# How the second batch's keys and queries are turned round: by TensorE, or as 32x32 blocks by VectorE

## The chip, the cores and the metric

The kernel runs on one core of one Trainium2 chip. The metric is the device time of one execution in microseconds (us); the figure used is the median over several runs. A profiled execution of the same kernel supplies the trace.

## The reference

For each of 8 batches and 8 heads, 32 pack vectors first attend to 576 keys, and then 576 queries attend to the 32 packed results. The heads' outputs form 4608 tokens of 512 features, and each token goes through a feed-forward layer whose nonlinearity is a quotient of polynomials.

```python
def sm_attn(qq, kk, vv):
    s = scale * np.matmul(qq, kk.transpose(0, 1, 3, 2))
    s = s - np.max(s, axis=-1, keepdims=True)
    a = np.exp(s)
    a = a / (np.sum(a, axis=-1, keepdims=True) + 1e-09)
    return np.matmul(a, vv)
p_packed = sm_attn(p, k, v)           # p: 8 x 8 x 32 x 64, k, v: 8 x 8 x 576 x 64
out = sm_attn(q, p_packed, p_packed)  # q: 8 x 8 x 576 x 64
x = out.transpose(0, 2, 1, 3).reshape(4608, 512)
h = x @ w_in                          # 512 x 2048
P = a[0] + a[1] * h + a[2] * h**2 + a[3] * h**3
Q = 1.0 + abs(b[0]) * abs(h) + abs(b[1]) * h**2
return (P / (Q + 1e-6)) @ w_out       # 2048 x 512
```

The weights of the feed-forward layer arrive as 64-bit floats and are brought to 32 bits on the chip.

## The kernel before, in words

**Tiling.** The feed-forward work is cut into 128 units: 8 batches, two halves of 288 tokens, and 8 chunks of 256 hidden features. A unit (`hidden`, L814) makes two tiles `h` on TensorE, evaluates the quotient on ScalarE, VectorE and GpSimd (tiles `Y`, `U`, `sq`, `V`), and leaves the result in `gh` and `gl`; three units later `acc_block` (L893) multiplies it with `w_out` into `acc`. In batch 0 the attention output `AH` is kept in plain 32 bits, and the first 12 units use plain 32-bit results too. From batch 1 on, operands are kept as two rounded parts and TensorE takes three products. While batch 0 is in work, the 64-bit weight words are still arriving and are converted (`convert`, L429, on ScalarE and VectorE).

**Attention.** `attention(bb)` (L548) is a generator of 16 steps. Batch 0 runs before the first unit. The steps of batch bb + 1 are handed out among the units of batch bb (L949 to L953), so batch 1's attention shares the engines with batch 0's units and with the weight conversion. Its steps: keys turned so that head features lie on the partitions (`transposed`, L569, called at L584), scores of the packs against the keys, softmax, the product with `v` (L683), the packed result transposed into `ppT` (L732, L733), queries turned (L736), scores of the queries against the packs, and the second softmax, whose result is `AH`.

**Two ways to load and turn keys and queries.** `rows4(bb)` (L464) chooses, and it is true for batches 0 and 1 in the kernel before.

- True: one DMA for each group of four heads brings 512 rows of a head as 128 partitions x 4 consecutive rows (L528); the last 64 rows of each head come apart, in tile `r` (L477, L490), which lives in a buffer of the ring `AH`. TensorE transposes 128x128 blocks into PSUM, and ScalarE copies them to `kx` (L574 to L581, L589 to L593, L738 to L744). The pack softmax is taken over two separate ranges of keys and joined afterwards with correction factors on VectorE and ScalarE (L647 to L657, L728 to L731).
- False: each group of four heads comes through four DMAs of 144 KB into 32 partitions each, made of single rows of 256 bytes (L513 to L518). VectorE transposes 32x32 blocks straight into `kx`, one instruction of 128x576 for two heads of a group (L570 to L573). All 576 rows come together, so tile `r` is not needed, and the two ranges share one maximum (L604 to L624), so the correction factors go.

`v` follows the row order: two DMAs of 256 KB instead of one of 512 KB a group (L509 to L511), four of 32 KB instead of two of 64 KB for its last rows (L499 to L501).

**What sets the order.** Nothing is issued as it stands in the source. `Planner` (L32) records all operations, gives each a cost (L40 to L48), simulates the engines in a list scheduler for four rounds, and issues the best order found. Every engine then works through its own queue strictly in that order. All DMAs are issued from SyncE (SP). The planner reckons a DMA at 600 ns of issue and with a rate by the length of the contiguous run: 190 bytes a nanosecond from 256 bytes on, and 370 from 1 KB on. In the first 150 us of the plan, TensorE's idle time is filled with small products of a zero tile (L992 to L1009), which add nothing.

The profile shows nearly all work under L226, the planner's issuing line, so groups are told apart by tile names.

Of the kernel before, what the change touches and what calls it, by code (L numbers as in the profile page):

```python
# [257 lines left out]
def attention_rational_ffn(  # L258
# [202 lines left out]


    NAT, AH, AL, PPT = {}, {}, {}, {}
    rows4 = lambda bb: bb < 2  # L464

    def load(bb, what):
        if bb >= B:
# [573 lines left out]
```

## Time and profile before

| | |
|---|---|
| median of 3 runs | 786.12 us (785.88 to 786.27) |
| profiled execution | 788.12 us |
| its span, from first to last instruction | 786.0 us |
| mean granted TensorE clock | 0.987 of full speed |
| TensorE / VectorE / ScalarE / GpSimd busy | 745.8 / 693.2 / 657.8 / 453.6 us |
| moved by DMA | 56.03 MB, mean 71 GB/s |

The busy shares are averages over stages that differ. The span has a start of some 50 us in which weights and the first batches arrive, then batch 0's units beside batch 1's attention up to about 150 us, then seven more batches of about 89 us each.

### The profile page before, as it was taken

The numbers are of one execution on the slowest core, as the hardware profiler recorded it, in microseconds if no ns is written. First come the engines' busy times: TensorE is split into PE (matmuls) and PEld (weight loads), VectorE is DVE, ScalarE is ACT, GpSimd is POOL, SyncE is SP. The second block draws the span as 40 slices with busy tenths as digits, with TensorE's granted clock in tenths as the row PEclk, the third lists the DMA queues.
The fourth block names the chain that finished last, engine by engine and source line by source line (L and its number), as shares of the span: only waits on it lengthen the run. The fifth ranks groups of instructions, "written<-read, shape, count | busy, mean of one in ns | idle before, by whom it ended". The sixth has DMA issues, their size and how long they took to land.

```text
span 786.0 us, 14945 instructions
## 1 busy us (share of the span) xinstructions
PE 745.8 (95%) x5336; PEld 567.5 (72%) x5336; DVE 693.2 (88%) x1295; ACT 657.8 (84%) x1464; POOL 453.6 (58%) x448
## 2 busy tenths in 40 slices
PE   2679999999999999999999999999999999999997
PEld 1345555588778887678778887678787887778886
DVE  4899999998999789998999789998999789988873
ACT  5869978988896998888897898889798788998872
POOL 0012448757585665756686555756587556766663
PEclk9959999999999999999999999999999999999999
DMA  9984353023601155023601136023701132000001
GB/s 297 332 296 143 108 100 49 1 85 46 110 1 55 45 66 90 1 85 46 95 17 55 44 52 104 1 58 62 94 28 54 41 45 46 1 22 7 27 1 41
DMA packets 152027, 56.03 MB, mean 71 GB/s; under 512 B 122256, under 2 KB 141200, under 8 KB 151952
## 3 DMA queue, kind: packets, MB, share of 16 engines
q1 hardware_dynamic: 151952, 55.07, 30.7%
q8 instruction: 42, 0.69, 0.4%
q14 instruction: 33, 0.27, 0.1%
HBM read 45.62 MB, written 9.44 MB: 70 GB/s over the span
## 4 chain that ended last, share of the span: by engine, by line
PE 76%; ACT 10%; DVE 8%; DMA 4%; issue 1%; POOL 0%; SPq 0%; DVEq 0%; ACTq 0%
PE acc L226 38%; PE h L226 24%; PE at L226 14%; DVE Y L226 4%; ACT Y L226 2%; DMA nat<-in_k_dram 2%; DVE w L226 2%; ACT V L226 1%; ACT U L226 1%; ACT sq L226 1%; ACT kx L226 1%; ACT w L226 1%; DMA m<-in_moe_w_in_dram 1%; ACT m L226 1%; DVE small L226 1%
## 5 line engine op out<-in xcount | busy, mean ns | idle before, releaser
L226 POOL TENSOR_TENSOR U<-U,sq 128x576 f32<-128x576 f32 x128 | 184.1, 1438 | 109.1 <-ACT U L226 55.8
L226 PE MATMUL acc<-w,gh 128*128 128x512 f32 x736 | 239.3, 408 | 1.6 <-ACT gh L226 1.4
L226 PE MATMUL h<-AH,m 128*128 128x288 f32 x1024 | 201.1, 320 | 7.9 <-DVE Y L226 5.6
L226 PEld LDWEIGHTS h<-AH,m 128*128 128x128 f32 x1024 | 163.0, 191 | 45.8 <-DVE Y L226 22.6
L226 POOL TENSOR_TENSOR gl<-Y,gh 128x512 fp32r<-128x512 f32 x116 | 150.2, 1295 | 39.0 <-issue 14.3
L226 PEld LDWEIGHTS acc<-w,gh 128*128 128x128 f32 x736 | 131.8, 188 | 45.5 <-issue 11.8
L226 PE MATMUL acc<-w,gl 128*128 128x512 f32 x384 | 147.9, 412 | 0.0
L226 ACT ACTIVATE Y<-h,abS 128x288 f32<-128x288 f32 x256 | 126.3, 511 | 23.2 <-PE h L226 19.7
L226 ACT ACTIVATE sq<-h 128x288 f32<-128x288 f32 x256 | 107.0, 419 | 39.2 <-PE h L226 31.0
L226 DVE TENSOR_TENSOR Y<-Y,h 128x288 f32<-128x288 f32 x256 | 109.1, 444 | 26.3 <-ACT Y L226 9.7
L226 DVE SCALAR_TENSOR_TENSOR Y<-Y,abS,h 128x288 f32<-128x288 f32 x256 | 124.5, 504 | 2.2
L226 DVE SCALAR_TENSOR_TENSOR Y<-Y,abS,V 128x576 f32<-128x576 f32 x128 | 102.8, 803 | 23.6 <-ACT V L226 23.0
L226 ACT ACTIVATE U<-h 128x288 f32<-128x288 f32 x256 | 98.6, 424 | 9.8 <-PE h L226 4.7
L226 ACT ACTIVATE V<-U,one 128x576 f32<-128x576 f32 x128 | 98.4, 769 | 5.6 <-DVE Y L226 3.8
L226 PE MATMUL h<-AL,m 128*128 128x288 f32 x448 | 96.1, 295 | 0.0
L226 DVE SCALAR_TENSOR_TENSOR V<-U,V 128x576 f32<-128x576 f32 x128 | 96.0, 750 | 0.0
L226 PEld LDWEIGHTS acc<-w,gl 128*128 128x128 f32 x384 | 71.9, 188 | 23.9 <-issue 9.6
L226 DVE SCALAR_TENSOR_TENSOR Y<-V,Y 128x576 f32<-128x576 f32 x116 | 86.7, 748 | 1.9
L226 POOL COPY G<-Y 128x64 f32<-128x64 f32 x116 | 27.5, 237 | 102.6 <-DVE Y L226 95.6
L226 ACT ACTIVATE V<-V 128x576 f32<-128x576 f32 x128 | 84.8, 663 | 0.7
L226 PE MATMUL acc<-half,gh 128*128 128x512 f32 x240 | 78.4, 413 | 1.3 <-ACT gh L226 0.9
L226 ACT CAST gh<-Y 128x512 fp32r<-128x512 f32 x116 | 73.4, 632 | 6.0 <-DVE Y L226 5.5
(135 smaller groups left out, 984.1 us busy)
## 6 DMA issues: line engine op xcount, KB each, us to landing
w<-in_moe_w_out_dram SPq DMA_DIRECT2D x16, 512.0 KB, 4.6
out_dram<-half SPq DMA_DIRECT2D x15, 512.0 KB, 3.1
nat<-in_k_dram SPq DMA_DIRECT2D x48, 144.0 KB, 3.9
nat<-in_q_dram SPq DMA_DIRECT2D x48, 144.0 KB, 4.3
nat<-in_v_dram SPq DMA_DIRECT2D x24, 256.0 KB, 3.7
m<-in_moe_w_in_dram SPq DMA_DIRECT2D x8, 512.0 KB, 6.2
w<-in_moe_w_in_dram SPq DMA_DIRECT2D x8, 512.0 KB, 8.2
nat<-in_k_dram SPq DMA_DIRECT2D x4, 512.0 KB, 7.7
```

What stands on the lines that cost most here:

```text
L226: getattr(getattr(self.nc, engine), name)(*args, **kwargs)
```

## The change

One number changes. Batch 1 takes the second way of loading and turning keys and queries, which batches 2 to 7 already take; only batch 0 keeps the first.

```diff
-    rows4 = lambda bb: bb < 2
+    rows4 = lambda bb: bb < 1
```

`rows4` is asked in `load`, `transposed`, `attention` and in the order of the output rows (L912), so all of what is described under "False" above now holds for batch 1. The planner then makes a new order for the whole kernel.

## Rows read from the trace of the kernel before

**Rows 1.** Page, part 4: the chain that ended last, by engine
```profile
PE 76%; ACT 10%; DVE 8%; DMA 4%; issue 1%; POOL 0%; SPq 0%; DVEq 0%; ACTq 0%
```
**Rows 2.** Windows by stage: busy us (and count) by engine, clock, DMA share, GB/s
```profile
core 0: us, PE busy (x) PEld busy (x) DVE busy (x) ACT busy (x) POOL busy (x), PEclk, DMA share, GB/s
48.00:88.00 40.00, 35.68 (x225) 18.48 (x225) 38.14 (x61) 37.89 (x80) 13.33 (x9) 0.86 0.54 185
88.00:110.00 22.00, 20.70 (x152) 12.07 (x151) 21.95 (x42) 17.43 (x37) 8.51 (x7) 1.00 0.31 99
110.00:153.00 43.00, 43.00 (x210) 23.08 (x210) 40.19 (x82) 38.62 (x84) 31.70 (x27) 1.00 0.28 41
153.00:190.00 37.00, 37.00 (x343) 30.00 (x342) 32.77 (x65) 34.12 (x82) 22.31 (x24) 1.00 0.15 46
```
**Rows 3.** Chain in order of time, start: start us, us, what
```profile
29.66 9.84 DMA nat<-in_k_dram
40.00 5.30 DMA w<-in_moe_w_in_dram
47.62 2.96 DVE w L226 x3
53.79 4.22 PE h L226 x8
```
**Rows 4.** Chain in order of time, batch 1's attention
```profile
59.14 0.48 ACT kx L226
65.63 0.30 ACT kx L226
96.75 0.07 DVE small L226
109.50 0.27 DVE small L226
109.81 0.66 PE at L226 x4
111.53 0.44 PE at L226 x4
112.83 0.44 PE at L226 x4
114.24 0.87 PE at L226 x8
```
**Rows 5.** Timeline of SP: start us, us, issue, count
```profile
28.16 2.00 SPq L226 DMA_DIRECT2D nat<-in_k_dram  x2
30.21 2.08 SPq L226 DMA_DIRECT2D AH<-in_k_dram  x1
32.40 2.13 SPq L226 DMA_DIRECT2D pn<-in_p_dram  x3
34.57 0.42 SPq L226 DMA_DIRECT2D AH<-in_q_dram  x1
35.51 0.31 SPq L226 DMA_DIRECT2D pn<-in_p_dram  x1
37.10 0.31 SPq L226 DMA_DIRECT2D AH<-in_q_dram  x1
39.57 0.90 SPq L226 DMA_DIRECT2D w<-in_moe_w_in_dram  x2
...
101.33 1.22 SPq L226 DMA_DIRECT2D nat<-in_q_dram  x2
...
112.00 6.76 SPq L226 DMA_DIRECT2D nat<-in_k_dram  x8
```
**Rows 6.** DMA of 101 to 108 us, queue: packets, MB, share of 16 engines
```profile
q1 hardware_dynamic: 1632, 1.18, 47.3%
```
**Rows 7.** DMA of 112 to 122 us, the same line
```profile
q1 hardware_dynamic: 9344, 1.18, 106.2%
```
**Rows 8.** Tile nat on VectorE: ns min/median/max, first and last start
```profile
L226 DVE STREAM_TRANSPOSE kx<-nat x48: 732/767/773, 150.7 to 657.9; 128x576 f32<-128x576 f32 x48
```
**Rows 9.** Timeline of ScalarE: start us, us, operation, idle before and releaser
```profile
45.39 1.19 ACT L226 ACTIVATE w<-w 128x1024 f32<-128x1024 f32 x1 [4.87 <-DMA w<-in_moe_w_in_dram]
```
**Rows 10.** Timeline of VectorE, the same columns
```profile
44.91 0.77 DVE L226 STREAM_TRANSPOSE AH<-kx 128x576 f32<-128x576 f32 x1
47.62 0.69 DVE L226 TENSOR_SCALAR w<-w 128x1024 int32<-128x1024 int32 x1 [1.36 <-ACT win L226]
```

**Rows 11.** Timeline of TensorE: start us, us, operation, count
```profile
63.77 0.60 PE L226 MATMUL at<-ident,AH 128*128 128x128 f32 x4
...
72.60 0.67 PE L226 MATMUL at<-kx,small 64*32 64x256 f32 x16
...
108.93 0.27 PE L226 MATMUL at<-ident,nat 128*128 128x128 f32 x1
...
121.42 0.72 PE L226 MATMUL at<-kx,ppT 64*32 64x288 f32 x16
```

## The prediction

> **What bounds the kernel now.** I first read the chain of waits by engine [rows 1]: TensorE holds 76% of it, so over the whole span the kernel is a TensorE kernel. But the change touches batch 1's attention alone, which lies in the first 150 us, so I next read the busy time by stage [rows 2]. From 48 to 88 us ScalarE (37.89 of 40) and VectorE (38.14) are both nearly full; from 88 to 110 VectorE is busy 21.95 of 22 us; from 110 on TensorE is busy without a gap, 43.00 of 43 and 37.00 of 37, while VectorE still has 40.19 of 43 and only after 153 some air (32.77 of 37). Thus the stage into which VectorE work is to be put is the one stage where VectorE has no room. Third comes the chain in order of time. At the start it runs through a DMA: batch 1's keys take 9.84 us from issue to landing, the next weight words only then start, and take 5.30 us more [rows 3]; ScalarE idles 4.87 us for those words [rows 9]. In the middle it passes through a few pieces of batch 1's attention on ScalarE and VectorE, and from 109.81 us on it is TensorE [rows 4].
>
> **The change part by part.**
>
> *TensorE.* 40 transposes of 128x128 go: 16 for keys, 4 for the keys' last rows, and the same again for queries. Eight of them take 0.87 us on the chain [rows 4], 0.109 us each. The 20 for keys are over at 64 us [rows 11], where TensorE was not the limit: worth nothing. Those for queries start at 108.93 us, and from 109.81 on TensorE is the limit: 20 x 0.109 = 2.2 us off the chain, if VectorE keeps up. The score products change by slivers (64 columns become 32), which I cost at nothing.
>
> *ScalarE.* 11 copies from PSUM go. Only two of those for keys stand on the chain, 0.48 and 0.30 us [rows 4], 0.78 together. VectorE is as full as ScalarE there, so I count half, 0.4.
>
> *VectorE.* Eight block transposes come, at 0.767 us [rows 8]: 4 for keys, 3.07 us, and 4 for queries, 3.07 us. Off go four tiny operations of the joined softmax, each about 0.08 us of chain (a neighbour shows 0.07), and two scalings of 0.27 us [rows 4]: 4 x 0.08 + 2 x 0.27 = 0.86 us, all in the stretch where VectorE is the limit. Net +5.3 us of VectorE work between 45 and about 120 us.
>
> The keys' transposes have one gap to hide in, the 1.36 us before 47.62 us [rows 10], if the keys have landed. Bounds: 0 to +3.07; I take 3.07 - 1.36 = +1.7, because that gap is the only one near their landing.
>
> The queries' transposes fall at about 110 us. If VectorE gets behind there, +3.07; if it fits them into the 2.8 us left of 43 [rows 2] and TensorE stays the limit, -2.2. I take the middle, +0.45: both engines are over 93% busy, so neither row is nearer.
>
> *The DMAs.* Batch 1's issues on SP grow from 15 to 28: keys 2 to 8, queries 2 to 8, `v` 2 to 4 and its last rows 2 to 4, while the three of tile `r` go and the four of `p` stay. Eight key issues of this form take 6.76 us of SP's time; the present two with the one of `r` behind them take 4.08 [rows 5]. The transfer matters more. 1.18 MB in the present form (queries of batch 1 and four small pieces of `v`) held the 16 engines for 0.473 x 7 = 3.3 us [rows 6]; the same 1.18 MB in 256-byte rows (keys of batch 2) held them for 1.062 x 10 = 10.6 us [rows 7]. Batch 1's keys take 3.3 us for the bulk plus about 1.2 us for the 0.13 MB of `r` (10.6 / 9), 4.5 us in all; they will take 10.6, or 6.1 us more, at a time when weight words queue behind them.
>
> How much of it is felt? The weight words issued at 39.57 us stand eight issues behind the second key DMA (issued at 29.66), which landed just before, at 39.50 [rows 3, 5]: SP seems to wait for the landing of the DMA eight places ahead. With eight key DMAs and four of `p` in front, the words would wait for the fifth key DMA. If key transfers begin at 39.5 - 4.5 = 35 us, it lands at 35 + 5/8 x 10.6 = 41.6, 2.1 us later. Bounds: 0 if the planner puts the words first, +6.1 if they wait for all of it. I take +2.0. Everything behind it waits: ScalarE's idle time [rows 9], the conversion on VectorE, the first chunks' products.
>
> Queries are issued at 101.33 us [rows 5] and will land some 7 us later than now (10.6 - 3.3), at about 113; the first products with them run at 121.42 [rows 11], so I cost that at nothing; without that cover, the queries' transposes would hold up VectorE's queue (conversions and unit work behind them), up to 7 us. The next batch's keys come correspondingly later, with over 25 us to spare (their first transposes are at 150.7 [rows 8]).
>
> The Trainium skill, "DMA: Bandwidth & Descriptors", section "Why small descriptors are slow (HBM only)", puts the loss of 256-byte pieces at a fixed 3 cycles on 8, or 27%. That does not agree with the 3.3 and 10.6 us above, a factor of 3.2. By its figure, an estimate, the keys would cost about 3.3 x 1.27 = 4.2 us, no more than now, and the start term would be 0.
>
> *The sum.* Start +2.0, keys on VectorE +1.7, ScalarE's copies -0.4, small operations -0.86, queries +0.45: +2.9 us. On the profiled execution, 788.12 + 2.9 = 791.0 us. That execution is 2.0 us above the median of the runs, so the median should be 786.12 + 2.9 = 789.0.
>
> **The rivals.**
>
> *Faster: TensorE and ScalarE shed work and VectorE hides its own.* The planner puts the weight words ahead of the keys and finds room for the transposes. For it: the chain from 109.81 us on is all TensorE, and there is slack before keys are used (the scores come at 72.60 us [rows 11]). Against it: VectorE's 21.95 of 22 us [rows 2]. -2.2 - 0.78 - 0.86 = -3.8, so 782.3 us. The Trainium skill, "VectorE: DVE Perf Modes", section "Rules for kernel authors", says as much: for 32x32 blocks the VectorE transpose is the fastest. The trace has 0.767 us for 576 columns, 0.17 for each 128, against 0.109 on TensorE, so per column it is not faster here; what speaks for it is the copy that ScalarE saves.
>
> *Nothing seen: the costs cancel.* Start and keys are hidden, and VectorE's delay at 110 us eats TensorE's 2.2: 786 us, within 1 us.
>
> *Much slower: VectorE's queue is blocked by a DMA.* Place: the keys' transposes, ordered before batch 0's last softmax operations and the conversion (VectorE's transposes into `AH` at 44.91 us, `w` at 47.62 [rows 10]). The planner reckons 256-byte rows at 190 bytes a nanosecond, 6.2 us for 1.18 MB, where [rows 7] shows 10.6. VectorE then stands at its queue's head for up to 4.4 us, and `AH`, the conversions and all products of `h` behind it wait. It decides as soon as the second group's transposes are ordered before about 46 us (35 + 10.6). Price: the full start term 6.1 and the whole VectorE addition 5.3: +11, 797 us. Against it: in later batches no VectorE transpose of `nat` shows a wait for its DMA.
>
> That the change does not act as described I rule out: batches 2 to 7 show this form in the trace [rows 8]. The new order of the whole plan can move the rest by a microsecond; TensorE is saturated after 150 us, which leaves little to move.
>
> **How the numbers follow.** Forecast 789.0: chance 0.40 (0.32 of it slower by over 0.2%, 0.08 within). Faster rival 0.25 (0.23 and 0.02). Nothing seen 0.20 (0.14 within, 0.03 on either side). Much slower 0.15. A measurement of this kernel tells about 0.2%, 1.6 us, from no change. Hence faster 0.26, same 0.24, slower 0.50. The range goes from 782.0, just below the faster rival, to 796.0, just short of the worst sum; the forecast's own is 786 to 793 (each of its two positive terms at zero, or the start at 6.1).
>
> **What would show it.** In the profile after: SP issues eight key DMAs near 28 us and the words of 39.57 us come 2 us later, ScalarE's idle time for them grows from 4.87 to about 7 us. VectorE busy rises by 5 us, 4.4 us less of TensorE's transposes and some 4 us less of ScalarE's copies (8 of 0.48 and 0.30). The chain between 60 and 110 us turns from ScalarE to VectorE. TensorE's unbroken stretch starts later than 109.8 us. The forecast is wrong if the words go ahead of the keys, if VectorE's addition sits in gaps that the present order doesn't show, or if a wait for `nat` stands ahead of VectorE's work.

## The result, and the profile after

The changed kernel takes 790.84 us (median of 5 runs, 789.34 to 791.28) against 786.12 us before. The ratio is 1.0049, with a 95% interval of 1.0036 to 1.0061: slower by half a per cent, 4.7 us. The forecast was 789.0. The two profiled executions are 791.01 and 788.12 us, 2.9 us apart: the one before lay 2.0 us above the median of its runs, the one after 0.2. A few executions below (839 to 2526 us) ran in a slower state of the chip; they count in the medians given, not in the ratios, and the traced one of "keys only" is among them, so that kernel has no row in the table of units.

The page of the changed kernel, part 1 (busy us, share of the span, instructions) and part 4 (the chain by engine):

```profile
PE 742.0 (94%) x5308; PEld 563.3 (71%) x5308; DVE 701.0 (89%) x1297; ACT 653.8 (83%) x1452; POOL 453.8 (57%) x448
...
PE 74%; DVE 12%; ACT 8%; DMA 2%; issue 2%; SPq 1%; POOL 0%; ACTq 0%; DVEq 0%
```

VectorE rose by 7.8 us and ScalarE fell by 4.0, TensorE by 3.8; the chain moved the same way, VectorE from 8% [rows 1] to 12%. The same stages as in [rows 2], now after the change:

```profile
48.00:88.00 40.00, 30.00 (x178) 15.45 (x177) 38.80 (x62) 36.95 (x71) 13.34 (x9) 0.81 0.63 212
88.00:110.00 22.00, 20.70 (x149) 11.61 (x147) 21.17 (x31) 15.16 (x30) 6.26 (x4) 1.00 0.40 87
110.00:153.00 43.00, 41.33 (x195) 20.63 (x196) 42.74 (x85) 36.65 (x77) 30.59 (x25) 1.00 0.40 51
153.00:190.00 37.00, 36.80 (x267) 29.74 (x266) 34.01 (x66) 33.18 (x81) 23.93 (x25) 1.00 0.15 46
```

VectorE (third engine column) is busy 42.74 of 43 us between 110 and 153, where it had 40.19, and TensorE (first) is no longer without gaps there. TensorE's granted clock in the stage from 48 to 88 us fell from 0.86 to 0.81; two experiments below that lose 4.0 and 7.5 us had 0.89 in that stage, so their loss is not the clock's. The chain of the changed kernel in order of time (start us, us, what) shows the turn: TensorE's unbroken stretch, which began at 109.81 [rows 4], is now reached at 119.54, is lost again to VectorE at 130.53, and holds from 145.70 on. VectorE holds the chain from 92.17 us:

```profile
92.17 0.46 DVE Y L226
...
111.25 1.32 DVE w L226
...
119.54 2.81 PE acc L226 x6
...
130.53 0.46 DVE kx L226
...
144.50 1.16 DVE Y L226 x3
145.70 2.21 PE h L226 x8
```

The start, SP's timeline as in [rows 5], and the rows of ScalarE and VectorE that answer to [rows 9, 10] (start us, us, operation, count, idle before):

```profile
24.84 12.86 SPq L226 DMA_DIRECT2D nat<-in_k_dram  x7
37.74 1.32 SPq L226 DMA_DIRECT2D w<-in_moe_w_out_dram  x2
39.11 0.43 SPq L226 DMA_DIRECT2D nat<-in_k_dram  x1
39.65 2.57 SPq L226 DMA_DIRECT2D pn<-in_p_dram  x4
42.31 0.90 SPq L226 DMA_DIRECT2D w<-in_moe_w_in_dram  x2
```
```profile
44.39 1.15 ACT L226 ACTIVATE w<-w 128x1024 f32<-128x1024 f32 x1 [1.17 <-DMA w<-in_moe_w_out_dram]
```
```profile
45.62 2.10 DVE L226 STREAM_TRANSPOSE kx<-nat 128x576 f32<-128x576 f32 x3
48.13 0.46 DVE L226 TENSOR_TENSOR Y<-Y,h 128x288 f32<-128x288 f32 x1 [0.42 <-ACT sq L226]
48.51 0.77 DVE L226 STREAM_TRANSPOSE kx<-nat 128x576 f32<-128x576 f32 x1
```

The words issued at 39.57 us before come 2.74 us later. The first words of `w_out` moved much further: the planner has put seven of the key loads ahead of them, and they are issued at 37.74 us, where the kernel before has them ahead of its keys:

```profile
25.23 1.70 SPq L226 DMA_DIRECT2D w<-in_moe_w_out_dram  x2
```

VectorE's hole of 1.36 us [rows 10] is gone: key transposes stand in it.

Where the time was lost is best read unit by unit. Every unit has one first activation of `V` on ScalarE; the table gives how much later its start is than in the kernel before (us, from the timelines of ScalarE, one execution each; the last column is the last unit). The runs of the kernel before alone spread from 785.2 to 789.9 us on one chip, so a difference of one or two us between two rows can't be read.

```
unit               0     2     4     6     8    10    13    15    18    24   127
after            1.1  -1.6  -0.1   1.5   1.6   3.8   5.9   5.6   3.3   2.9   3.4
queries only     2.0   0.6   1.5   0.1   0.6   1.9   2.3   3.0   0.1   0.8   0.8
row loads       -1.0  -0.9   3.8   1.9   2.5   2.4   3.2   3.7   2.8   2.7   2.9
vector work     -0.9  -1.1   4.4   2.5   3.5   6.2   5.6   6.3   4.5   5.7   5.6
long key loads   2.3   1.7   5.1   1.6   1.8   4.0   3.6   3.3   2.1   2.7   2.4
after, words 1st 2.9   2.4   4.6   5.0   2.9   4.4   4.8   5.3   3.3   4.0   4.1
same order long  2.5   0.6   2.1   3.7   3.8   6.0   8.1   7.8   5.5   5.1   5.5
before, 2nd plan 0.2  -2.1  -2.2  -1.8  -3.0  -1.6  -0.7  -0.9  -4.0  -3.5  -3.1
```

In the changed kernel units 1 to 4 are not late. The delay builds up between units 4 and 13 (86 to 151 us), reaches 5.9 us, falls to 2.9 by unit 24, and stays near that. Every row of the table gains between units 15 and 18 (0.9 to 3.1 us), whatever its change: part of that fall belongs to the kernel before, or to its one traced execution.

How full VectorE is until unit 15 is told by one window per kernel, from 34 us to the start of that unit's activation. First the kernel before:

```profile
34.00:156.31 122.31, 112.37 (x678) 61.22 (x677) 116.24 (x213) 106.35 (x221) 54.55 (x43) 0.92 0.43 122
```
And after:
```profile
34.00:161.88 127.88, 111.33 (x665) 58.60 (x662) 125.27 (x219) 104.78 (x212) 54.56 (x43) 0.91 0.52 126
```

Before, VectorE was idle for 122.31 - 116.24 = 6.1 us of this stretch, after for 2.6. It is busy 9.0 us longer by then: 3.5 us of that went into idle time, 5.6 became delay. What it does more can be told by form (operation, count, busy us, mean ns). The groups of transposes and of one step of the weight conversion, first before, then after:

```profile
L226 DVE STREAM_TRANSPOSE kx<-nat 128x576 f32<-128x576 f32 x2 | 1.5, 767 | 0.0
L226 DVE SCALAR_TENSOR_TENSOR w<-w 128x1024 int32<-128x1024 int32 x11 | 13.8, 1264 | 0.0
```
```profile
L226 DVE STREAM_TRANSPOSE kx<-nat 128x576 f32<-128x576 f32 x11 | 8.2, 760 | 0.0
L226 DVE SCALAR_TENSOR_TENSOR w<-w 128x1024 int32<-128x1024 int32 x11 | 15.5, 1409 | 0.0
```

Nine more transposes (eight of batch 1, one of batch 2 that now comes before unit 15) are 6.7 us. The same eleven conversion steps took 1.7 us longer, which the forecast did not have; why they did is not shown.

### The profile page after: what moved, and what is told of

The parts are those of the page before. It is cut to its first block, busy times and chain, and to the rows that moved or that the text cites. A ratio compares the mean times of both kernels' runs of the same rounds, so it can differ in the third digit from the quotient of the medians.

```text
span 789.3 us, 14893 instructions
## 1 busy us (share of the span) xinstructions
PE 742.0 (94%) x5308; PEld 563.3 (71%) x5308; DVE 701.0 (89%) x1297; ACT 653.8 (83%) x1452; POOL 453.8 (57%) x448
## 4 chain that ended last, share of the span: by engine, by line
PE 74%; DVE 12%; ACT 8%; DMA 2%; issue 2%; SPq 1%; POOL 0%; ACTq 0%; DVEq 0%
PE acc L226 37%; PE h L226 24%; PE at L226 13%; DVE Y L226 5%; DVE w L226 3%; ACT Y L226 2%; DMA nat<-in_k_dram 2%; DVE small L226 1%; ACT U L226 1%; ACT sq L226 1%; DMA AH<-in_k_dram 1%; ACT kx L226 1%; DVE V L226 1%; SPq L226 1%; ACT V L226 1%
## 5 line engine op out<-in xcount | busy, mean ns | idle before, releaser
L226 PEld LDWEIGHTS acc<-w,gl 128*128 128x128 f32 x384 | 71.7, 188 | 26.0 <-issue 11.8
```

Source lines behind the costliest of these rows:

```text
L226: getattr(getattr(self.nc, engine), name)(*args, **kwargs)
```

## The experiments

Theory 1: VectorE's added work is the loss, because VectorE has no room in batch 0's stage. Theory 2: the loads in small pieces hold up the weight words. Theory 3: any new plan moves the time by as much. All ratios are against runs of the kernel before on the same chip. Except under "The same order", each kernel below also has a new order from the planner, so what it shows of a cost includes that of its order.

**Keys only.** A second switch for the queries, so that batch 1's keys alone take the new way.

```diff
-    rows4 = lambda bb: bb < 2
+    rows4 = lambda bb: bb < 1      # keys, v, pack softmax
+    rows4q = lambda bb: bb < 2     # queries, order of the output rows
```

> Only batch 1's keys (with v and the pack softmax) take the new way; its queries stay with TensorE. Theory 1 (VectorE has no room in batch 0's stage): +3.07 us of key transposes, less the 1.36 us gap before 47.6 us, less 0.86 us of small operations: +0.9, so 786 to 788 us. Theory 2 (the loads in small pieces): the keys are the ones that queue ahead of weight words, so most of the loss is here, 788 to 791. Theory 3 (the loss is only what any new plan gives): no number, as likely below as above 786.

Measured: 792.54 us, ratio 1.0063 (1.0048 to 1.0079). The whole loss is seen with the keys (and `v` and the pack softmax, which change with them). Theory 1's number (at most 788) is missed by over 4 us; theory 2's (up to 791) is just passed.

**Queries only.** The two bounds exchanged.

> Only batch 1's queries take the new way. Theory 1: 3.07 us more on VectorE at about 110 us, where it is full, and 2.2 us less on TensorE that cannot be used while VectorE is behind: 788 to 790 us. Theory 2: at 100 to 115 us the DMA engines are mostly free, so the loads cost nothing and TensorE's 2.2 us are gained: 784 to 786.

Measured: 787.67 us, ratio 1.0004 (0.9994 to 1.0014). The queries' part costs nothing that can be measured, between the two expectations. Units 13 to 15 are 2.3 to 3.0 us late, as theory 1 has it, and 0.8 is left by unit 24.

**Row loads, TensorE transposes.**

```diff
+        if bb == 1 and x != "v":
+            t = nat_ring.next()
...          # the four DMAs of the new way into t
+            NAT[bb, what] = t[:, 0 : 4 * NS * D].rearrange("p (h s d) -> p h s d", h=4, s=NS)
+            return
```

> The kernel before, but batch 1's keys and queries are loaded in the small pieces of the new way (8 DMAs of 144 KB each) while TensorE still transposes and ScalarE copies; what it then computes for batch 1 is in the wrong order. Theory 1: the loads are covered, 786 us within 1. Theory 2: the whole loss, 789 to 792.

Measured: 791.09 us, ratio 1.0050 (1.0037 to 1.0063): the loads, with no VectorE work added, cost nearly as much as the change (4.0 of 4.7 us). Theory 2's number. The loads of tile `r` (256 KB) stay in this kernel, which the change takes out. Its `w_out` words are late as in the changed kernel (issued from 37.71 us on). Until its unit 15, 3.7 us late, VectorE is idle for 125.96 - 117.82 = 8.1 us, 2.1 more than before, in waits for units that come late; the other 1.6 us are operations that took longer or were put earlier:

```profile
34.00:159.96 125.96, 111.53 (x681) 60.74 (x674) 117.82 (x216) 106.53 (x222) 54.80 (x43) 0.95 0.51 128
```
```profile
48.43 0.46 DVE L226 TENSOR_TENSOR Y<-Y,h 128x288 f32<-128x288 f32 x1 [2.55 <-ACT sq L226]
52.73 0.46 DVE L226 TENSOR_TENSOR Y<-Y,h 128x288 f32<-128x288 f32 x1 [2.29 <-ACT sq L226]
```

**VectorE work alone.** Each copy of batch 1's keys and queries into `kx` is preceded by a VectorE transpose into the same place.

```diff
+                if bb == 1:
+                    flat_n = NAT[bb, f"{x}{g}"].rearrange("p h s d -> p (h s d)")
+                    n = flat_n[:, 512 * r : 512 * r + 512].rearrange("p (j c) -> p j c", j=2)
+                    nc.vector.transpose(to[:, r, 2 * g : 2 * g + 2, :], n)
```

> The kernel before, with 8 VectorE block transposes of 128x512 added in batch 1's attention, 4 from the keys' tiles and 4 from the queries' (some 5.5 us of VectorE), whose results are overwritten; loads, TensorE and ScalarE as before. Theory 1: the whole loss or more, 790 to 792 us, because TensorE keeps its transposes. Theory 2: 786 within 1.

Measured: 794.63 us, ratio 1.0098 (1.0083 to 1.0112), 7.5 us: more than theory 1 asked. VectorE is full in the stages that follow:

```profile
48.00:88.00 40.00, 31.87 (x219) 16.61 (x218) 38.48 (x59) 36.64 (x76) 13.32 (x8) 0.89 0.54 180
88.00:110.00 22.00, 21.75 (x165) 12.45 (x158) 22.00 (x43) 16.84 (x35) 7.69 (x5) 1.00 0.33 105
110.00:153.00 43.00, 40.48 (x186) 20.95 (x185) 42.70 (x82) 35.99 (x76) 30.23 (x25) 1.00 0.25 40
```

So the loads alone lose 4.0 us and VectorE work alone 7.5, and the change, which has both, 4.7: they do not add. The comparison is not clean: the added transposes also delay ScalarE's copies behind them, which the changed kernel doesn't have, and TensorE keeps its transposes.

**Long key loads.** The changed kernel with batch 1's keys loaded per group in one DMA of 512 KB and two of 32 KB.

> The kernel after, but batch 1's keys are loaded in long pieces (per group one DMA of 512 KB and two of 32 KB); VectorE still does the block transposes, so what is computed for batch 1 is wrong. Theory 1 (VectorE's added work is the loss): no change against the kernel after, about 1.005 of before. Theory 2 (the key loads hold up the weight words): the loss goes, 0.998 to 1.001 of before. Both, as two ways to use up the same VectorE time: a part stays, 1.002 to 1.004.

Measured: 789.01 us, ratio 1.0017 (1.0004 to 1.0031): some two thirds of the loss go when the planner may reckon with cheap key loads. Its order is then another one: `w_out`'s first words stand ahead of the keys again.

```profile
25.41 1.71 SPq L226 DMA_DIRECT2D w<-in_moe_w_out_dram  x2
28.34 6.50 SPq L226 DMA_DIRECT2D nat<-in_k_dram  x6
```

So it is not shown whether the gain is the transfer's or the order's.

**Words first.** An edge for the planner: key loads of batch 1 wait for the issue of two sets of words. First on the kernel after, then on the one before.

```diff
+            if "in_k" in x.tensor.name and x.offset // (8 * 576 * 64) == 1:
+                edges[i].update(words)   # DMAs of w_out chunk 0 and w_in chunk 6
```

> The kernel after, with one edge added for the planner: batch 1's key loads are not issued before the weight words of the first w_out chunk and the seventh w_in chunk. The same work and the same bytes in another order on SP. Theory 1: as the kernel after, 1.005 of before. Theory 2: the words come in time, 0.998 to 1.001. Both: 1.002 to 1.004.

> The kernel before with the same added edge. Theory 1: no change, 1.000. Theory 2: its key loads hold up the words too (ScalarE idles 4.87 us for them), so 0.995 to 0.999. If another order of SP alone moves the time by half a per cent either way, theory 3 (any new plan) gains.

Measured: 793.04 us, ratio 1.0074 (1.0049 to 1.0100), and 789.90 us, ratio 1.0038 (1.0025 to 1.0050). Theory 2 in its simple form falls: with the words in front the time does not get better. The kernel before gets worse; the kernel after can't be told from 1.0049, as the intervals overlap. The second result speaks for theory 3 by its own expectation: an edge that adds no work, only another order, costs 0.38% (0.25 to 0.50), nearly as much as the change. In the first kernel, SP issues the keys from 41.46 us on, and VectorE takes their transposes at 56 to 63 us, in the full stage instead of the hole:

```profile
41.46 10.93 SPq L232 DMA_DIRECT2D nat<-in_k_dram  x8
```
```profile
56.42 1.43 DVE L232 STREAM_TRANSPOSE kx<-nat 128x576 f32<-128x576 f32 x2
...
61.94 1.42 DVE L232 STREAM_TRANSPOSE kx<-nat 128x576 f32<-128x576 f32 x2
```

**The same order, one cost removed.** These three keep the changed kernel's order instruction for instruction on every engine and exchange calls only when they are issued. The first reads one contiguous stretch per partition for each of the eight key DMAs; the second makes plain copies of the eight transposes; the third does both.

```diff
+            name, args = swap(engine, name, args)
             getattr(getattr(self.nc, engine), name)(*args, **kwargs)
```

> The kernel after with its order kept instruction for instruction; only the eight key loads of batch 1 read one contiguous stretch per partition instead of 36 pieces of 128 bytes (same 144 KB each, same target, wrong data). It takes the loads' form alone out, with no new plan. Theory 2: the loss goes, 1.000 of before or less. Theory 1: unchanged, 1.005. Both: in between, 1.002 to 1.004.

> The kernel after with its order kept instruction for instruction; only the eight block transposes of batch 1 become plain copies of the same 128x576 on VectorE, which I expect to take about half the time (some 3 us less VectorE work in all; the data are then not transposed). Theory 1: the time falls by nearly as much, to 1.001 to 1.002 of before. Theory 2: unchanged, 1.005.

> Both of the last two at once, the order kept. If the two costs add up: below before, 0.997 to 0.999. If they stand in for one another (a late load leaves VectorE a hole that the transposes fill), less than the sum of the two, 0.999 to 1.001.

Measured: 792.84 us, ratio 1.0070 (1.0058 to 1.0083); 792.20, ratio 1.0062 (1.0050 to 1.0074); 792.67, ratio 1.0067 (1.0054 to 1.0080). Not one of them gains, and the expectation for the third (at most 1.001) is missed whichever way the two costs combine. For the loads the answer is plain: with this order the form of the key loads is not what costs. The key issues go faster (seven in 8.52 us instead of 12.86), but words of `w_in` issued just ahead of them take 12.23 us to land, SP waits for them, and `w_out`'s are issued at 36.38, hardly earlier than 37.74 (first a line of the chain, then SP's timeline):

```profile
24.13 12.23 DMA w<-in_moe_w_in_dram
```
```profile
25.29 8.52 SPq L241 DMA_DIRECT2D nat<-in_k_dram  x7
36.38 1.63 SPq L241 DMA_DIRECT2D w<-in_moe_w_out_dram  x2
```

From unit 2 on this kernel's units are the changed kernel's shifted by 2.2 us, and its VectorE is as full, which fits a pace set by the order of VectorE's queue. The shift is not the loads': the kernel with copies, whose loads are the changed kernel's, lies 1.8 us behind it from unit 10 on. The changed kernel itself was not run beside these three. The second experiment failed to remove its cost. The copies came out nearly as long as the transposes (ns min/median/max), so it says nothing against theory 1:

```profile
L238 DVE COPY kx<-nat x8: 452/630/1181, 46.9 to 126.1; 128x576 f32<-128x576 f32 x8
```

**Other plans.** The planner's time for a signal between engines from 200 to 220 ns, in both kernels.

```diff
-    PASS = 200
+    PASS = 220
```

> A control: the kernel before, planned with 220 instead of 200 ns for a signal from one engine to another; the same work, another order. Theories 1 and 2: within 0.2% of before. Theory 3 (any new plan moves the time as much as the change did): off by 0.4% or more.

> A control: the kernel after, planned with 220 instead of 200 ns for a signal from one engine to another, as was done with the kernel before (which gave 0.998). Theories 1 and 2: within 0.2% of the kernel after, 1.003 to 1.007 of before. Theory 3: anywhere from 0.998 to 1.010.

Measured: 786.31 us, ratio 0.9984 (0.9971 to 0.9997), and 789.45 us, ratio 1.0026 (1.0015 to 1.0038). This new plan moves either kernel by about 0.2%, and under it the change costs 1.0026 / 0.9984 = 1.0042, where it cost 1.0049 under the first. That speaks against theory 3 as the whole loss. It doesn't rule it out: the edge of "words first" moved the kernel before by 0.38%, and two plans of each kernel are few. The first of the two is also, by its ratio, the fastest kernel of this study.

## Why the prediction was right, and where its steps were off

- **Direction and bound: right.** VectorE was named as the engine without room, and in the trace after it holds the chain from 92 to 119.5 and from 130.5 to 145.7 us; before it did from 89 to 109.8. Its added work shows in the page: +7.8 us, where 5.3 were counted. The eight transposes are 5.9 of it (42.4 us against 36.5 for all of this form); the twelve conversion steps of one form took 16.7 us instead of 15.0, which was not in the sum. VectorE's total differs from plan to plan as well: the kernel before has 693.2 us, its second plan 695.7.
- **Start, +2.0: the delay came, the way to it and the place of the cost were wrong.** The words were issued 2.74 us later (2.1 forecast). They did not wait for the fifth key DMA to land: SP was busy without a gap, and seven key issues alone took 12.86 us, where [rows 5] has 6.76 for eight. Nor are units 1 to 4 late. ScalarE's wait for words fell from 4.87 to 1.17 us where 7 had been forecast (with its waits for TensorE it still idles about as long, 4.5 us between 40 and 47 us), because the planner moved `w_out`'s words and the first chunks' products.
- **An input of the start term was misread.** The share of 47.3% in [rows 6] belongs to the 9 us from 101 to 110 us; for 101 to 108 it is 60.8%:

```profile
q1 hardware_dynamic: 1632, 1.18, 60.8%
```

Either way the packets took 4.3 us, not 3.3. The present key loads come to about 5.4 us instead of 4.5, the row form is slower by a factor of 2.5 and not 3.2, and the start term worked out in the same way would be +1.2 and not +2.1. The 10.6 us are also a sum of packet times, some of which must overlap: 106.2% is more than a window of 10 us holds. With the right share the forecast would have been about 788, further from 790.84.
- **Keys on VectorE, +1.7: hidden at their place, the loss appears later.** They stand at 45.6 to 49.3 us, in the time in which a late load left VectorE without work. Row loads alone cost 4.0 us, VectorE work alone 7.5, the change 4.7: the two terms that the sum adds do not add. A reading that fits is that each fills the same hole, and that what the hole took is paid for by a full VectorE queue after 86 us; no run isolates this, since the experiment that was to take out both at once left the VectorE time where it was.
- **Queries, +0.45: right within the noise.** Queries alone: +0.04% (-0.06% to +0.14%), with 2.3 us lost at unit 13 and most of it given back, as every kernel of the table does between units 15 and 18. Their later loads were covered, as assumed.
- **ScalarE, -0.4 and the small operations, -0.86:** not tried apart. ScalarE's copies did go (-4.0 us busy).
- **The rivals.** "Faster" fails where it was said to: VectorE had no room. "Nothing seen" fits the queries alone, but not the change. "Much slower" did not come: VectorE never waited for a key load. Its reasoning had an error. The pieces are not rows of 256 bytes, as the text ahead of the prediction says, but half rows of 128 (L517 takes 32 of 64 features; [rows 7] has 9344 packets for 1.18 MB). The planner therefore reckons 100 bytes a nanosecond, 11.8 us for 1.18 MB, close to the 10.6 measured, so it was not too hopeful about the landing. What the Trainium skill's "DMA: Bandwidth & Descriptors" says under "Why small descriptors are slow (HBM only)" was for 256-byte pieces. The rows have pieces half as long, so their factor of 2.5 can't be set against it.
- **From the profile to the median.** Profile to profile the sum of +2.9 was met exactly, but medians are 4.7 apart: the single profiled execution before lay 2.0 us above its median, and taking that as constant put the forecast 1.8 us too low. The agreement of the sum is in good part chance: its largest term rests on a misread share and was not seen at its place, the next was hidden where it stands, and the loss built up between units 4 and 13, where the sum has only the queries' term.

What stays open: how the 4.7 us divide between the late words, VectorE's work and the order that the planner made around them; and why the delay falls from 5.9 to 2.9 us after unit 13. TensorE's missing transposes (3.8 us less busy) would explain it, and the vector-work kernel, which keeps them, gives nothing back between units 13 and 24 (5.6 and 5.7); but the second plan of the kernel before keeps them too and gains 2.9 us on the first between the same units, so this was not shown.

## What to carry to other kernels

Read the stage into which the work goes before counting what it costs: an engine that is idle elsewhere can be full there, as VectorE was here at 95% and more. The price need not be the work's length, though: 5.5 us of added VectorE work alone cost 7.5, while 3 us for the queries, which took 20 transposes off TensorE in the same stretch, cost nothing measurable. Two costs can each lose about as much alone as together, so undo them separately and together before blaming either, and make sure that the edit takes the cost out: a copy was hardly cheaper than the transpose that it replaced. Where a planner orders everything, keep the order fixed in one experiment, with the unchanged kernel run beside it, and change the order without the work in another: here the order alone was worth 0.2 to 0.4%, the change 0.4 to 0.5% under either plan, so the order is not a small correction.

## What the runs showed of the hardware that was not expected

A plain VectorE copy of 128x576 in 32 bits took 630 ns in the median (452 to 1181), against 758 ns (735 to 779) for the 32x32 block transpose of the same tiles in the changed kernel: in the median, the transpose is nearly as cheap as a copy here.
